# Table limits read from PSUM, second weights of expert 0 split later, gate copies deferred, and a new order of the first matmul groups

## The chip, the cores and the metric

The kernel runs on one core of a Trainium2 chip. The metric is the device time of one execution in microseconds; lower is better. TensorE (PE) does the matmuls, VectorE (DVE), ScalarE (ACT) and GpSimd (POOL) the work on elements, and SyncE (SP) issues most DMA transfers. Each engine goes through its own instructions in a fixed order and waits on semaphores for what other engines or DMA queues deliver.

## The reference, cut to what matters

Attention over 8 batches of 8 heads (576 tokens, head size 64) in which only scores within tau of the row's maximum are kept, then a mixture of 8 experts in which each of the 4608 tokens goes to one:

```python
scores = scale * np.matmul(q, k.transpose(0, 1, 3, 2))
thresh = np.max(scores, axis=-1, keepdims=True) - tau
scores = np.where(scores >= thresh, scores, -1000000000.0)
attn = softmax(scores)
x = (attn @ v), heads side by side            # 4608 x 512
logits = x @ w_gate                           # 4608 x 8
expert_idx = np.argmax(logits, axis=1)
for e in range(8):
    xe = x[expert_idx == e]
    h = np.maximum(xe @ w1[e], 0.0)           # 512 -> 1024
    out[expert_idx == e] = gate_w * (h @ w2[e])   # 1024 -> 512
```

## The kernel before

Everything large is held as a pair of 16-bit floats, a high part and a low part, and each product is made of three matmuls. A "split" writes the high part (ACT) and the low part (DVE: the value less its high part).

**Attention** goes through 32 pairs of heads, numbered n, each in 11 steps. In a step PE makes scores twice: `s` with tokens in rows (L356, L358), of which DVE takes the row maximum `nm` (L368), and for an earlier pair `st`, transposed (L404, L405), which ACT turns into `e` by the exponential (L421), DVE masks (L424), ACT rounds to `ph` (L429) and POOL takes the rest of into `pl` (L430). `av` (L474) multiplies `ph` and `pl` with the values `vop`. All `s` and `st` share six PSUM buffers, `av` has one, and one more PSUM buffer (tag "m") serves the small jobs. After four pairs, which are one batch, ACT copies the sums to `x` and `xh` (L484, L489), POOL normalises them (`xn`, L528), ACT and POOL split them into rows `R` (L535, L536), SP transposes `R` by DMA into `xTg` (L543), PE makes the logits `lg` (L561) and the ranks `rk` within an expert (L610 to L613), and POOL scatters the rows to a table `xs` in DRAM (L633, "put").

**Tables.** After batches 5, 6 and 7 `tables0`, `tables1` and `tables2` work out which rows of `xs` belong to which block of 128 tokens (m) of which expert. `counts` (L660) lets PE count the tokens (`pc`, a PSUM bank), DVE writes the counts less a base to `cnt` in SBUF (L665). `table_first` (L668) takes from `cnt` the limits `lim` (L681) and the flag `has` (L689), and works in the bank to the end, where `row` and `badi` come out as integers (L658).

**Experts.** `fetch(m)` gathers 128 rows by an indirect DMA of POOL (`Rm` or `R`<-`xs`, L847), has SP transpose them into `xTm` (L857), and copies the gate and the target of each row into `gt` (DVE L860, POOL L865). `gemm1` of a group of blocks makes `h` (L902) and ACT and DVE its split `hl` (L890, L891), `gemm2` makes `y` (L935); ACT scales it to `o` (L946), and POOL writes it out (L949). The blocks of expert 0 that `tables0` gives (m = 0, 1, 2) are computed as groups 0, 1, 2 while attention still goes on and right behind it; matmuls named h<-spare belong to group 3, which is made of spare rows. Weights come by SP (`wf`, L791) and are split by `split_w` (ACT L806, DVE L814). For expert 0 the low part of a weight goes through PE: a matmul with the identity puts the high part into PSUM (`hi_w`, L254), and DVE subtracts it from there (L255). Expert 0 has two `wf` buffers, the later ones eight, loaded from `close` on.

**Order.** `plan(k, f)` queues a piece for step k of attention, `after(d, f)` for d steps later, `moe(c, ready, f)` for chunk c of the expert work when a condition holds, and `hurry(f)` gives a piece's instructions high priority. A scheduler puts the instructions of each engine in order by priority and dependency. `experts` runs the groups: first weights of group i, then second weights of group i-1, and so on.

Of the kernel before, what the change touches and what calls it, by code (L numbers as in the profile page):

```python
# [50 lines left out]
def kernel(  # L51
# [123 lines left out]
    def plan(k, f, where=END):  # L175
        if urgent[0]:
            f = hurry(f)
        assert (k, where) >= (now[0], slot[0])
        acts.setdefault(k, ([], [], []))[where].append(f)
# [481 lines left out]
    def counts(nm):  # L661
        pc = ps_m.tile([P, 512], F32, tag="m", name=f"pc_{nm}")
        nc.tensor.matmul(pc[:, 0:E], ones, run, start=True, stop=True)
        c = tp.tile([P, E], F32, name=f"cnt_{nm}")
        nc.vector.tensor_tensor(c, pc[:, 0:E], base_e, ALU.subtract)  # L665
        return c, pc

    def table_first(nm, bank, cnt, start=None):  # L668

        bc = [P, E, NE]  # L670
        if start is None:
            rk_i = tp.tile(bc, I32, name="rk_i")
            nc.gpsimd.iota(rk_i, pattern=[[0, E], [P, NE]], base=0, channel_multiplier=1)
            nc.vector.tensor_copy(rk_f, rk_i)
        rk, bad = (bank[:, z:z + E * NE].rearrange("p (e n) -> p e n", e=E) for z in (32, 96))
        if start is None:
            nc.scalar.copy(rk, rk_f)
        else:
            nc.vector.tensor_tensor(rk, rk_f, start.unsqueeze(2).to_broadcast(bc), ALU.add)
        lim = tp.tile([P, E, 1], F32, name=f"lim{nm}")  # L680
        nc.vector.tensor_scalar(lim[:, :, 0], cnt, -1.0, None, ALU.add)  # L681
        nc.vector.tensor_tensor(bad, rk, lim.to_broadcast(bc), ALU.is_gt)
        nc.vector.tensor_scalar(bad, bad, float(1 << 20), None, ALU.mult)
        badi = to_int(bad, bc, f"badi{nm}")
        nc.vector.tensor_tensor(rk, rk, lim.to_broadcast(bc), ALU.min)
        nc.vector.tensor_tensor(rk, rk, base_e.unsqueeze(2).to_broadcast(bc), ALU.add)

        has = tp.tile([P, E, 1], F32, name=f"has{nm}")
        nc.vector.tensor_scalar(has[:, :, 0], cnt, 0.5, None, ALU.is_gt)  # L689
        nc.vector.scalar_tensor_tensor(rk, rk, pos0, has.to_broadcast(bc), ALU.subtract, ALU.mult)  # L690
        nc.vector.tensor_scalar(rk, rk, pos0, None, ALU.add)
        rowi = to_int(rk, bc, f"row{nm}")
        return rowi, badi
# [76 lines left out]
    groups += [(m, m + 1) for m in range(NPR, NEARLY, 2)]  # L770
    groups += [(m,) for m in range(NEARLY, NS)]
    group_of = {m: (g, i) for g in groups for i, m in enumerate(g)}
    ms = {}
    wq = {}
    T = {}
# [43 lines left out]
    def fetch(m):  # L819

        idx, bad, par = slots[m]
        g, i = group_of[m] if m != "x" else ((m,), 0)
        if m in range(NF, NF + 2):

            if "spare" not in T:
                T["spare"] = xp.tile([P, 2, NT * H * W // 2], F32, tag="x", name="spare")
            Rm = T["spare"][:, m - NF, 0:ROW].bitcast(I32)
            xT = T["spare"][:, m - NF, 520:1032].bitcast(F16).rearrange("p (i c t) -> p i c t", i=1, c=8)
        elif m in range(EARLY_SLOTS):
            Rm = pools[0].tile([P, ROW], I32, tag="Rm", name=f"Rm_{m}", bufs=2)  # L830
            xT = pools[0].tile([P, 1, 8, P], F16, tag="xTm", name=f"xTm_{m}", bufs=NF)
        else:
            Rm = R[:, 0 if m == "x" else m % 5]
            if i == 0:
                xT = rpool.tile([P, 2, 8, P], F16, tag="xT", name=f"xTm_{m}", bufs=3)
            else:
                xT = ms[g]["xT"]
        if i == 0:
            ms[g] = dict(xT=xT, par=par, gw=[], ti=[])
        d = ms[g]  # L840
        for z in range(1 + late(m)):
            dst = xT[:, i]
            if late(m):
                Rm = R[:, z if m == "x" else (2 * m + z) % 5]
                dst = xT.rearrange("p i c t -> p (i c t)")[:, 0:8 * PL].rearrange("p (c t) -> p c t", c=8)
                d["xT"], dst = dst, dst[:, :, P * z:P + P2 * z]
            get = nc.gpsimd.indirect_dma_start(  # L847
                Rm, None, xs[:, :], bass.IndirectOffsetOnAxis(ap=idx[:, z:z + 1].bitcast(U32), axis=0)
            )
            get = get.ins  # L850
            mine = [put for b, put in puts if b <= placed.get(m, B - 1)]
            for put in mine:
                tc.add_manual_dep(get, put.name, sync, reason="rows of the tokens placed so far")
            if m != "x":
                tc.declare_no_dep(get, group="puts", keep=mine, reason="rows of tokens placed later are others")
                tc.add_to_no_dep_group("gets", get)
            nc.sync.dma_start_transpose(dst, Rm[0:P2 if z else P, 0:DM].bitcast(F16))  # L857
            gt = small.tile([P, 2], I32, tag="gt", name=f"gt_{m}_{z}", bufs=6)
            gw, ti = gt.bitcast(F32)[:, 0:1], gt[:, 1:2]
            nc.vector.tensor_copy(gw, Rm.bitcast(F32)[:, DM:DM + 1])  # L860
            to = Rm[:, DM + 1:DM + 2]
            if z:
                nc.gpsimd.tensor_tensor(ti, to, to, ALU.add)
                to = ti
            nc.gpsimd.tensor_tensor(ti, to, bad[:, z:z + 1], ALU.add)  # L865
            d["gw"].append(gw)
            d["ti"].append(ti)

    def shape(g):

# [3 lines left out]
    def chunks(g):  # L874

        return 8 * shape(g)[1] // P

    def gemm1(g):
        d = ms[g]
        Wt, xT = wb1[d["par"]].rearrange("p c (h f) -> p c h f", h=2), d["xT"]  # L880

        n, w, per = shape(g)
        d["h"] = []

        def relu(ph, u):
            if u % 2 == 0:
                d["h"].append(ew.tile([P, 2, 2, 512], F16, tag="e", name=f"hl_{g[0]}_{u}"))
            h = d["h"][u // 2][:, :, u % 2, 0:per * w]
            ph = ph[:, 0:per * w]
            nc.scalar.activation(h[:, 0], ph, AF.Relu)  # L890
            nc.vector.scalar_tensor_tensor(h[:, 1], ph, 0.0, h[:, 0], ALU.max, ALU.subtract)  # L891

        for u in range(8 // per):
            ph = ps_sc.tile([P, 512], F32, tag="sc", name=f"h_{g[0]}_{u}")
            k = 0
            for q in range(per):
                f = slice((per * u + q) * P, (per * u + q + 1) * P)
                o = ph[:, q * w:(q + 1) * w]
                for c in range(4):
                    for z, (wh, xh) in enumerate(((0, 0), (0, 1), (1, 0))):  # L900
                        x = xT[:, 2 * c + xh] if late(g[0]) else xT[:, 0:n, 2 * c + xh]
                        nc.tensor.matmul(  # L902
                            o, Wt[:, c, wh, f], x, start=c == 0 and z == 0, stop=c == 3 and z == 2,
                        )
                        k += w
                        if k >= 12 * P and (q, c, z) != (per - 1, 3, 2):
                            k -= 12 * P
                            yield
            moe(chunk[0] + DH, lambda: True, lambda ph=ph, u=u: relu(ph, u))
            yield  # L910
# [3 lines left out]
    def gemm2(g):  # L914
        d = ms[g]
        Wt = wb2[d["par"]].rearrange("p c (a h d) -> p (c a) h d", a=2, h=2)
        n, w, per = shape(g)
        for i in range(len(d["ti"])):
            m = g[0] if late(g[0]) else g[i]

            half = late(m) and i
# [135 lines left out]

    def experts():

        for i in range(len(groups) + 1):  # L1060
            if i < len(groups):
                assert there(groups[i], 0)
                yield from gemm1(groups[i])
                past[0] = groups[i][-1]
            if i:
                assert there(groups[i - 1], 1)
                yield from gemm2(groups[i - 1])
                past[1] = groups[i - 1][-1]

    def room():  # L1070
        ldp.close()
# [11 lines left out]
    k = NSTEP * (NPAIR - 2) - LEAD - SL  # L1083
    plan(k + 1, room)
    for i in range(8):
        plan(k + WS0 + WSD * i, lambda i=i: split_w(*wseq[i]))
        if i + 2 < 8:
            plan(k + WS0 + WSD * i, lambda i=i: load_w(*wseq[i + 2]))
    TABLES = {B - 3: tables0, B - 2: tables1, B - 1: tables2}
    plan(KEND + 12, close)  # L1090


# [7 lines left out]

    at = []
    k = 0
    for i, g in enumerate(groups):
        at.append(k)
        k += chunks(g) + (chunks(groups[i - 1]) if i else 0)
    for i, g in enumerate(groups):
        for j, m in enumerate(g):
            if m >= NF + 2:
# [29 lines left out]
    def there(g, w):  # L1138

        e = g[0] // NE if g[0] < NEARLY else E + g[0] - NEARLY  # L1140
        return all((e, w, c) in split_done for c in range(4))
# [149 lines left out]
```

## Time and profile before

| | |
|---|---|
| three timed runs | 992.12, 993.51, 993.37 us; median 993.37 |
| profiled execution | 992.38 us |
| its span, first to last instruction | 990.7 us |
| PE busy | 939.0 us (95% of the span) |
| DVE, ACT, POOL busy | 702.8, 652.3, 561.6 us |
| mean granted PE clock | 0.987 of full |

Attention takes the span up to about 587 us; the expert work is woven into it from about 566 us and alone behind it. PE is busy nearly all the time, so what matters is where it is not: the start, the last fifty microseconds of attention, and the first seventy behind it.

### The profile page before, as it was taken

The numbers are of one execution on the slowest core, as the hardware profiler recorded it, in microseconds if no ns is written. First come the engines' busy times: TensorE is split into PE (matmuls) and PEld (weight loads), VectorE is DVE, ScalarE is ACT, GpSimd is POOL, SyncE is SP. The second block draws the span as 40 slices with busy tenths as digits, with TensorE's granted clock in tenths as the row PEclk, the third lists the DMA queues.
The fourth block names the chain that finished last, engine by engine and source line by source line (L and its number), as shares of the span: only waits on it lengthen the run. The fifth ranks groups of instructions, "written<-read, shape, count | busy, mean of one in ns | idle before, by whom it ended". The sixth has DMA issues, their size and how long they took to land. (4 is left out here: it accounts for less than half of the span.)

```text
span 990.7 us, 28651 instructions
## 1 busy us (share of the span) xinstructions
PE 939.0 (95%) x11548; PEld 604.1 (61%) x11548; DVE 702.8 (71%) x1413; ACT 652.3 (66%) x1111; POOL 561.6 (57%) x470
## 2 busy tenths in 40 slices
PE   7899999999999999999897898999999999999997
PEld 2355556556566556565564586777667766667684
DVE  7899999998999989999899875826243342423650
ACT  2689897997998889898988973534243342433651
POOL 6366886895996987978968871433122121221121
PEclk8899999999999999999999999999999999999999
DMA  6553554564564755646646639998574656556730
GB/s 199 143 132 80 146 134 125 140 164 112 127 179 115 162 125 141 171 94 170 152 97 188 149 104 289 363 228 250 164 232 115 216 151 180 171 155 209 224 105 27
DMA packets 142750, 159.20 MB, mean 161 GB/s; under 512 B 96403, under 2 KB 112789, under 8 KB 142614
## 3 DMA queue, kind: packets, MB, share of 16 engines
q1 hardware_dynamic: 126598, 100.33, 40.2%
q10 hardware_dynamic: 6768, 27.55, 8.9%
q0 software_dynamic: 9248, 29.45, 8.9%
q8 instruction: 92, 1.51, 0.7%
q14 instruction: 44, 0.36, 0.1%
HBM read 90.24 MB, written 19.44 MB: 111 GB/s over the span
## 5 line engine op out<-in xcount | busy, mean ns | idle before, releaser
L430 POOL TENSOR_TENSOR pl<-e,ph 128x1024 f16<-128x1024 f32 x158 | 335.9, 2134 | 105.1 <-ACT ph L429 66.6
L421 ACT ACTIVATE e<-st,ntau 128x512 f32<-128x512 f32 (+1 forms) x352 | 222.5, 650 | 54.2 <-PE st L405 51.5
L424 DVE SCALAR_TENSOR_TENSOR e<-st,e 128x512 f32<-128x512 f32 (+1 forms) x352 | 219.7, 635 | 12.2 <-ACT e L421 11.4
L935 PE MATMUL y<-wb,hl 128*128 128x512 f16 (+1 forms) x1056 | 201.8, 360 | 0.0
L368 DVE TENSOR_REDUCE nm<-s 128x1 f32<-128x512 f32 x300 | 188.1, 632 | 19.1 <-PE s L358 16.8
L902 PEld LDWEIGHTS <-wb 128*128 128x128 f16 x2304 | 188.2, 98 | 19.8 <-issue 1.2
L902 PE MATMUL h<-xTm,wb 128*128 128x256 f16 (+2 forms) x2112 | 195.2, 253 | 0.7 <-DMA xTm<-R 0.7
L474 PE MATMUL av<-vop,ph 128*128 128x65 f16 (+3 forms) x3072 | 187.7, 195 | 2.3 <-ACT x L484 2.0
L474 PEld LDWEIGHTS <-ph 128*128 128x128 f16 (+1 forms) x3072 | 158.3, 100 | 46.3 <-issue 21.3
L474 PE MATMUL av<-vop,pl 128*128 128x65 f16 (+1 forms) x1536 | 167.5, 194 | 4.6 <-POOL pl L430 4.5
L429 ACT CAST ph<-e 128x1024 f16<-128x1024 f32 x160 | 166.2, 1040 | 5.3 <-DVE e L424 5.0
L474 PEld LDWEIGHTS <-pl 128*128 128x128 f16 (+1 forms) x1536 | 136.6, 100 | 35.8 <-issue 10.5
L935 PEld LDWEIGHTS <-hl 128*128 128x128 f16 (+1 forms) x1056 | 94.0, 100 | 97.9 <-issue 1.9
L814 DVE SCALAR_TENSOR_TENSOR wb<-wf,wb 128x1024 f16<-128x1024 f32 x88 | 103.9, 1220 | 52.0 <-ACT wb L806 51.9
L404 PE MATMUL st<-QK 128*128 128x512 f16 (+3 forms) x640 | 138.8, 294 | 1.9 <-DVE lo L255 0.8
L405 PE MATMUL st<-CQ,ck 128*128 128x512 f16 (+3 forms) x640 | 137.4, 288 | 0.0
L356 PE MATMUL s<-QK 128*128 128x512 f16 (+1 forms) x600 | 129.6, 293 | 3.1 <-DMA QK<-hi 2.0
L358 PE MATMUL s<-ck,CQ 128*128 128x512 f16 (+1 forms) x600 | 128.0, 289 | 1.2 <-DMA CQ<-hi 1.2
L949 POOL DMA_INDIRECT out_dram<-o,gt x40 | 46.6, 1165 | 129.9 <-ACT o L946 118.8
L890 ACT ACTIVATE hl<-h 128x512 f16<-128x512 f32 (+1 forms) x80 | 45.6, 572 | 105.6 <-PE h L902 103.6
L806 ACT ACTIVATE wb<-wf 128x1024 f16<-128x1024 f32 x96 | 97.4, 1049 | 26.9 <-DMA wf<-in_w_dram 10.7
L860 DVE COPY gt<-R 128x1 f32<-128x1 f32 x33 | 5.1, 153 | 129.0 <-DMA out_dram<-o,gt 105.8
(194 smaller groups left out, 1016.6 us busy)
## 6 DMA issues: line engine op xcount, KB each, us to landing
wf<-in_w_dram SPq DMA_DIRECT2D x96, 512.0 KB
qkf<-in_qk_dram ACTq DMA_DIRECT2D x30, 576.0 KB
vf<-in_v_dram ACTq DMA_DIRECT2D x15, 640.0 KB
QK<-hi SPq DMA_DIRECT2D x64, 144.0 KB
QK<-lo SPq DMA_DIRECT2D x64, 72.0 KB
QK<-hi SPq DMA_DIRECT2D x64, 72.0 KB
ck<-lo SPq DMA_DIRECT2D x64, 72.0 KB
CQ<-hi SPq DMA_DIRECT2D x64, 64.0 KB
```

The costliest lines, as they stand in the source:

```text
L356: nc.tensor.matmul(sc[rows, oc], d["QA"][a][:, cols], d["KB"][a][:, CH[c]], start=True, stop=False)
L358: nc.tensor.matmul(sc[rows, oc], d["CQ"][:, at:at + cols.stop - cols.start], d["CK"][a][:, CH[c]], start=False, stop=True,)
L368: nc.vector.tensor_reduce(o, sc[:, 0:width(t)], axis=AX.X, op=ALU.max, negate=True)
L404: nc.tensor.matmul(sc[rows, oc], d["KB"][a][:, cols], d["QA"][a][:, CH[c]], start=True, stop=False)
L405: nc.tensor.matmul(sc[rows, oc], d["CK"][a][:, cols], d["CQ"][:, q], start=False, stop=True)
L421: nc.scalar.activation(pf, sc, AF.Exp, bias=ntau, scale=0.125 / SS)
L424: nc.vector.scalar_tensor_tensor(pf, sc, 0.0, pf, ALU.is_ge, ALU.mult)
L429: nc.scalar.copy(h, pd)
L430: (nc.vector if (n, t) in PLV else nc.gpsimd).tensor_tensor(l, pd, h, ALU.subtract)
L474: nc.tensor.matmul(av[:, 0:D] if z == 2 else av, l if z == 1 else h, vop[:, tv, W:W + D] if z == 2 else vop[:, tv, 0:W], start=i in (0, NT ...
L902: nc.tensor.matmul(o, Wt[:, c, wh, f], x, start=c == 0 and z == 0, stop=c == 3 and z == 2,)
L935: nc.tensor.matmul(o, h[:, hh], Wt[:, f, wh, c], start=f == 0 and z == 0, stop=f == 7 and z == 2)
```

## The change

Five edits:

1. `counts` writes the counts less the base into columns 8 to 15 of the PSUM bank, and ACT copies them to `cnt`. `lim` and `has` read the bank instead of `cnt`.
2. The four pieces of the second weights of expert 0 are split two steps apart from step KEND+1, behind the last pair's scores, instead of in attention. The loads of the last two pieces move with them. Low parts go through PSUM as before.
3. `tables0` is hurried.
4. The copies to `gt` are made later: 8 steps later for m below 5, otherwise 12 chunks later.
5. The groups run in the order `turns`: first weights of groups 0, 1 and 2, then second weights of 0 and 1, first of 3, second of 2, and then one by one as before.

```diff
@@ counts
-        nc.vector.tensor_tensor(c, pc[:, 0:E], base_e, ALU.subtract)
+        nc.vector.tensor_tensor(pc[:, 8:8 + E], pc[:, 0:E], base_e, ALU.subtract)
+        nc.scalar.copy(c, pc[:, 8:8 + E])
         return c, pc
@@ table_first
-        nc.vector.tensor_scalar(lim[:, :, 0], cnt, -1.0, None, ALU.add)
+        nc.vector.tensor_scalar(lim[:, :, 0], bank[:, 8:8 + E], -1.0, None, ALU.add)
...
-        nc.vector.tensor_scalar(has[:, :, 0], cnt, 0.5, None, ALU.is_gt)
+        nc.vector.tensor_scalar(has[:, :, 0], bank[:, 8:8 + E], 0.5, None, ALU.is_gt)
@@ groups
+    turns = [(1, 0), (1, 1), (1, 2), (0, 0), (0, 1), (1, 3), (0, 2)]
+    turns += [(w, i + w) for i in range(3, len(groups)) for w in (1, 0) if i + w < len(groups)]
@@ fetch
-            gt = small.tile([P, 2], I32, tag="gt", name=f"gt_{m}_{z}", bufs=6)
-            gw, ti = gt.bitcast(F32)[:, 0:1], gt[:, 1:2]
-            nc.vector.tensor_copy(gw, Rm.bitcast(F32)[:, DM:DM + 1])
...
+            def gates(Rm=Rm, z=z):
+                gt = small.tile([P, 2], I32, tag="gt", name=f"gt_{m}_{z}", bufs=6)
+                gw, ti = gt.bitcast(F32)[:, 0:1], gt[:, 1:2]
+                nc.vector.tensor_copy(gw, Rm.bitcast(F32)[:, DM:DM + 1])
...
+            if m == "x":
+                gates()
+            elif m < NF + 2:
+                after(8, gates)
+            else:
+                moe(chunk[0] + 12, lambda: True, gates)
@@ experts
-        for i in range(len(groups) + 1):
-            if i < len(groups):
-                assert there(groups[i], 0)
-                yield from gemm1(groups[i])
-                past[0] = groups[i][-1]
-            if i:
-                assert there(groups[i - 1], 1)
-                yield from gemm2(groups[i - 1])
-                past[1] = groups[i - 1][-1]
+        for first, i in turns:
+            assert there(groups[i], 1 - first)
+            yield from (gemm1 if first else gemm2)(groups[i])
+            past[1 - first] = groups[i][-1]
@@ weights of expert 0, tables
     for i in range(8):
-        plan(k + WS0 + WSD * i, lambda i=i: split_w(*wseq[i]))
+        t = k + WS0 + WSD * i if i < 4 else KEND + 1 + 2 * (i - 4)
+        plan(t, lambda i=i: split_w(*wseq[i]))
         if i + 2 < 8:
-            plan(k + WS0 + WSD * i, lambda i=i: load_w(*wseq[i + 2]))
-    TABLES = {B - 3: tables0, B - 2: tables1, B - 1: tables2}
+            plan(t, lambda i=i: load_w(*wseq[i + 2]))
+    TABLES = {B - 3: hurry(tables0), B - 2: tables1, B - 1: tables2}
```

DVE, where `tables0` begins during pairs 29 and 31. Names end in a number of the program, wb1_0 are the first weights of expert 0, and pc_0 is the bank of `tables0`. Before:

```order
L665 TENSOR_TENSOR cnt_0_12157<-pc_0_12155,base_e_109 128x8
L255 SCALAR_TENSOR_TENSOR wb1_0_11668<-wf_0_2_0_11829,hi_w0_2_0_12039 128x512
L255 SCALAR_TENSOR_TENSOR wb1_0_11668<-wf_0_2_0_11829,hi_w0_2_1_12051 128x512
L681 TENSOR_SCALAR lim0_12163<-cnt_0_12157 128x8
L689 TENSOR_SCALAR has0_12171<-cnt_0_12157 128x8
L368 TENSOR_REDUCE nm_31_11905<-s_31_5_12089 128x1
L255 SCALAR_TENSOR_TENSOR vop_1_128<-vf_15_11717,hi_v15_0_0_12093 128x5x64
```

Now:

```order
L665 TENSOR_TENSOR pc_0_12152<-pc_0_12152,base_e_109 128x8
L255 SCALAR_TENSOR_TENSOR wb1_0_11668<-wf_0_2_0_11829,hi_w0_2_0_12039 128x512
L255 SCALAR_TENSOR_TENSOR wb1_0_11668<-wf_0_2_0_11829,hi_w0_2_1_12051 128x512
L368 TENSOR_REDUCE nm_31_11905<-s_31_5_12089 128x1
L255 SCALAR_TENSOR_TENSOR vop_1_128<-vf_15_11717,hi_v15_0_0_12093 128x5x64
L255 SCALAR_TENSOR_TENSOR vop_1_128<-vf_15_11717,hi_v15_0_1_12100 128x5x64
L368 TENSOR_REDUCE nm_31_11905<-s_31_6_12110 128x1
L255 SCALAR_TENSOR_TENSOR wb1_0_11668<-wf_0_3_0_11915,hi_w0_3_0_12114 128x512
L424 SCALAR_TENSOR_TENSOR e_29_8_12001<-st_29_9_12071,e_29_8_12001 128x512
L682 TENSOR_SCALAR lim0_12161<-pc_0_12152 128x8
```

The limit reads PSUM, and stands six instructions later, behind two row maxima of pair 31; `has0` is not among these rows any more.

POOL, in the stretch behind that, up to the first gathers. Before:

```order
L528 TENSOR_TENSOR xn_6_3_12177<-x_6_10436,rs_6_11881 128x512
L430 TENSOR_TENSOR pl_29_8_12003<-e_29_8_12001,ph_29_8_12002 128x1024
L536 TENSOR_TENSOR R_129<-xn_6_2_12121,R_129 128x4x128
L430 TENSOR_TENSOR pl_29_4_12108<-e_29_4_12106,ph_29_4_12107 128x1024
L536 TENSOR_TENSOR R_129<-xn_6_3_12177,R_129 128x4x128
L430 TENSOR_TENSOR pl_29_6_12203<-e_29_6_12201,ph_29_6_12202 128x1024
L847 DMA Rm_0_12225<-xs_81,row0_12175 128x514
L847 DMA Rm_1_12272<-xs_81,row0_12175 128x514
L430 TENSOR_TENSOR pl_30_0_12335<-e_30_0_12333,ph_30_0_12334 128x1024
```

Now:

```order
L528 TENSOR_TENSOR xn_6_3_12175<-x_6_10436,rs_6_11881 128x512
L430 TENSOR_TENSOR pl_29_8_12003<-e_29_8_12001,ph_29_8_12002 128x1024
L430 TENSOR_TENSOR pl_29_4_12108<-e_29_4_12106,ph_29_4_12107 128x1024
L536 TENSOR_TENSOR R_129<-xn_6_2_12118,R_129 128x4x128
L536 TENSOR_TENSOR R_129<-xn_6_3_12175,R_129 128x4x128
L430 TENSOR_TENSOR pl_29_6_12201<-e_29_6_12199,ph_29_6_12200 128x1024
L430 TENSOR_TENSOR pl_30_0_12318<-e_30_0_12316,ph_30_0_12317 128x1024
L850 DMA Rm_0_12214<-xs_81,row0_12173 128x514
L850 DMA Rm_1_12258<-xs_81,row0_12173 128x514
```

The rest of pair 30's first scores, pl_30_0, now stands ahead of both gathers instead of behind them.

PE, where the logits of the last batch, lg_7, begin behind attention; h_2 and y_1 are the two products of groups 2 and 1, and lg_7 is made of five pieces of 12 matmuls. Before:

```order
L902 LDWEIGHTS wb1_0_11668
L902 MATMUL h_2_0_13474<-xTm_2_12351,wb1_0_11668 128x128
L561 LDWEIGHTS xTg_7_0_13425
L561 MATMUL lg_7_13511<-wg_107,xTg_7_0_13425 128x8
L561 LDWEIGHTS xTg_7_0_13425
```

Now:

```order
L947 LDWEIGHTS hl_1_0_13336
L947 MATMUL y_1_0_13630<-wb2_0_11669,hl_1_0_13336 128x512
L561 LDWEIGHTS xTg_7_0_13430
L561 MATMUL lg_7_13566<-wg_107,xTg_7_0_13430 128x8
L561 LDWEIGHTS xTg_7_0_13430
```

Between the end of attention's last av and lg_7 stood 84 matmuls h and 24 y, and the five pieces lay apart, with h and y between them. Now 144 h and 33 y stand ahead, and the five pieces follow each other.

## Rows read from the trace of the kernel before

**Rows 1.** The page: its first line, and busy time (share of span) and instructions of PE.

```profile
span 990.7 us, 28651 instructions
PE 939.0 (95%) x11548; PEld 604.1 (61%) x11548; DVE 702.8 (71%) x1413; ACT 652.3 (66%) x1111; POOL 561.6 (57%) x470
```

**Rows 2.** Windows: length, busy us per engine PE PEld DVE ACT POOL, clock, DMA share.

```profile
537.40:546.00 8.60, 4.58 (x14) 1.09 (x12) 8.60 (x13) 4.38 (x7) 6.96 (x7) 0.80 0.71 177
...
566.00:587.00 21.00, 21.00 (x491) 18.91 (x491) 13.57 (x34) 15.81 (x33) 16.15 (x12) 1.00 0.22 68
587.00:612.00 25.00, 22.39 (x301) 15.99 (x294) 15.04 (x32) 10.53 (x20) 7.17 (x10) 1.00 1.01 255
...
655.00:984.00 329.00, 329.00 (x2542) 229.65 (x2539) 127.54 (x168) 130.39 (x172) 75.80 (x96) 1.00 0.59 173
```

**Rows 3.** Waits of PE, 500 to 660 us: us in total, times, longest.

```profile
PE hi_w L254 <- DVE nm L368: 4.0, 1, 4.0
PE hi_w L254 <- ACT wb L806: 2.8, 3, 1.4
PE hi_v L254 <- ACT vop L286: 2.3, 1, 2.3
PE lg L561 <- DMA xTg<-R: 1.5, 3, 0.6
PE rk L610 <- DVE run L602: 1.1, 1, 1.1
PE h L902 <- DMA xTm<-R: 0.7, 1, 0.7
```

**Rows 4.** Timeline of DVE: start, us, engine, line, operation.

```profile
536.80 4.29 DVE L681 TENSOR_SCALAR lim<-cnt 128x8 f32<-128x8 f32 x1
...
547.46 0.17 DVE L658 CAST badi<-pc 128x32 int32<-128x32 f32 x1
```

**Rows 5.** Timeline of POOL; in brackets the idle time ahead and what ended it.

```profile
536.71 2.28 POOL L536 TENSOR_TENSOR R<-xn,R 128x512 f16<-128x512 f32 x2
538.94 2.12 POOL L430 TENSOR_TENSOR pl<-e,ph 128x1024 f16<-128x1024 f32 x1
...
542.50 2.05 POOL L528 TENSOR_TENSOR xn<-x,rs 128x512 f32<-128x512 f32 x2
546.30 2.13 POOL L430 TENSOR_TENSOR pl<-e,ph 128x1024 f16<-128x1024 f32 x1 [1.75 <-ACT ph L429]
548.54 1.16 POOL L536 TENSOR_TENSOR R<-xn,R 128x512 f16<-128x512 f32 x1
...
555.17 1.01 POOL L847 DMA_INDIRECT Rm<-xs,row  x1 [0.15 <-PE av L474]
```

**Rows 6.** Timeline of ACT.

```profile
543.66 0.69 ACT L421 ACTIVATE e<-st,ntau 128x512 f32<-128x512 f32 x1 [3.77 <-PE st L405]
...
549.31 1.06 ACT L806 ACTIVATE wb<-wf 128x1024 f16<-128x1024 f32 x1
```

**Rows 7.** Timeline of PE: the first h, and the end of attention.

```profile
565.69 0.38 PE L405 MATMUL st<-CQ,ck 128*128 128x512 f16 x1
565.90 0.83 PE L902 MATMUL h<-xTm,wb 128*128 128x128 f16 x12
...
587.19 2.85 PE L902 MATMUL h<-xTm,wb 128*128 128x128 f16 x48
589.88 5.34 PE L935 MATMUL y<-wb,hl 128*128 128x512 f16 x24
```

**Rows 8.** Timeline of SP, whose rows are DMA issues.

```profile
558.59 3.36 SPq L857 DMA_TRANSPOSE xTm<-Rm  x2
...
615.69 25.54 SPq L791 DMA_DIRECT2D wf<-in_w_dram  x15
643.88 6.72 SPq L857 DMA_TRANSPOSE xTm<-R  x2
```

**Rows 9.** A window as in the second group; the last but one number is the DMA share.

```profile
563.60:564.70 1.10, 1.10 (x34) 0.87 (x33) 0.93 (x6) 1.10 (x3) 1.08 (x3) 1.00 0.01 2
```

More of the change, by code (lines that the diff above doesn't have):

```diff
@@ L857, in fetch @@
             nc.sync.dma_start_transpose(dst, Rm[0:P2 if z else P, 0:DM].bitcast(F16))
-            gt = small.tile([P, 2], I32, tag="gt", name=f"gt_{m}_{z}", bufs=6)
-            gw, ti = gt.bitcast(F32)[:, 0:1], gt[:, 1:2]
-            nc.vector.tensor_copy(gw, Rm.bitcast(F32)[:, DM:DM + 1])
[L861 to L867, printed above, removed]
+            def gates(Rm=Rm, z=z):
+                gt = small.tile([P, 2], I32, tag="gt", name=f"gt_{m}_{z}", bufs=6)
+                gw, ti = gt.bitcast(F32)[:, 0:1], gt[:, 1:2]
+                nc.vector.tensor_copy(gw, Rm.bitcast(F32)[:, DM:DM + 1])
+                to = Rm[:, DM + 1:DM + 2]
+                if z:
+                    nc.gpsimd.tensor_tensor(ti, to, to, ALU.add)
+                    to = ti
+                nc.gpsimd.tensor_tensor(ti, to, bad[:, z:z + 1], ALU.add)
+                d["gw"].append(gw)
+                d["ti"].append(ti)
+            if m == "x":
[4 more added lines that the diff above has]
+                moe(chunk[0] + 12, lambda: True, gates)
     def shape(g):
@@ L917, in gemm2 @@
         n, w, per = shape(g)
-        for i in range(len(d["ti"])):
+        for i in range(2 if late(g[0]) else len(g)):
             m = g[0] if late(g[0]) else g[i]
@@ L1102 @@
     k = 0
-    for i, g in enumerate(groups):
-        at.append(k)
-        k += chunks(g) + (chunks(groups[i - 1]) if i else 0)
+    for begin, i in turns:
+        if begin:
+            at.append(k)
+        k += chunks(groups[i])
     for i, g in enumerate(groups):
```

## The prediction

> **What bounds the kernel now.** I read the page first: PE is busy for 939.0 of 990.7 us [rows 1], so at most 52 us are to be had, and the question is where they lie. The windows answer it. From 655 us to the end PE is busy in 329.00 of 329.00 us, and so it is in the last 21 us of attention [rows 2]: an edit that takes nothing from PE's own work gains nothing there. The idle time is in the stretch around 540 us (4.58 busy of 8.60) and right behind attention (22.39 of 25.00) [rows 2]. The list of PE's waits names what ended it: one wait of 4.0 us for a row maximum of DVE, 2.8 us in three waits for splits of weights by ACT, 2.3 us for ACT's split of the values; and behind attention 1.5 us in three waits for the transposed xTg, 1.1 us for the running counts and 0.7 us for a transposed xTm [rows 3]. The start-up, where PE also waits, is changed by one copy of a few elements, and I give it nothing.
>
> The 4.0 us have one origin. DVE's timeline shows `lim`, an operation on 8 elements per row, lasting 4.29 us from 536.80 to 541.09 [rows 4]. In all that time POOL works without a break, on two R and one pl, from 536.71 to 541.06 [rows 5], and `lim` ends when POOL ends. So it isn't working but held, by POOL. A DVE operation that reads PSUM isn't: the cast at 547.46 took 0.17 us while POOL was in a pl from 546.30 to 548.43 [rows 4, 5]. The row maxima queued behind `lim` then hold the shared PSUM buffers, PE can't write, and ACT stands for 3.77 us until 543.66 [rows 6]. PE pays a second time: its clock over 537.4 to 546 is granted at 0.80 of full [rows 2], so 40% of 8.6 us, 3.4 us, were at the lower of its two levels, 1.2 GHz; what it did in them would have taken half, so 1.7 us are lost.
>
> The Trainium skill ("SBUF — State Buffer", section "SBUF: two separate sides") says that VectorE and GpSimd share a pair of ports under a lock that is held for one whole instruction, the other blocking fully. Were the hold only to the end of the one POOL instruction under way, it would have ended within the first R, 1.2 us, and the edit would be worth 3 us less at this place; the trace shows it lasting across three instructions, 4.29 us, and I go by that.
>
> **The change part by part.**
>
> *Limits from PSUM.* `lim` now reads PSUM, like the cast: 0.17 us in place of 4.29 [rows 4]. Bounds: 0.17, and, if something else in it is held, what POOL's run leaves when it comes. It stands six instructions later, which would be about 540.0, so 1.1 us to 541.06. The added copies by ACT are on 8 columns, three in all. Bounds: nothing, and 0.69 us, the shortest ACT row that I show [rows 6]. I take some 0.2 us; the first falls into the time in which ACT waited 3.77 us. DVE, PE and ACT then go on some 3.8 us sooner, at PE's full clock.
>
> *Second weights behind the last pair.* This moves four ACT operations of 1.06 us [rows 6], 4.2 us at most; consecutive rows overlap by about a tenth, so I take 3.8 us; eight low parts on DVE; and eight PE matmuls of 512 columns, 5.34/24 = 0.22 each [rows 7], so 1.7 us. Two of PE's waits for splits (2.8 us in all, of which the first, for a first weight, stays) go with them, 2.0 us. ACT has room at the new place: 15.81 of 21.00 us busy [rows 2], so the 3.8 us are hidden; without that cover they would stand on the path of the last av. The 1.7 us are not hidden, since PE is full there; they come off the earlier stretch and go onto this one. The loads of the last two pieces need a buffer that the first two free. A load costs SP 25.54/15 = 1.70 us at its pace [rows 8], so each is ready some 3 us after the split that frees it, against some 6 us of matmuls that the new order puts between the first and the third on PE: 0 to 0.6 us of waiting, I take 0.3.
>
> *What is next late.* One would now add 4.0 + 1.7 + 2.0 + most of 2.3 us. I don't, because POOL comes next. Its 1.75 us of idleness ahead of 546.30 [rows 5] goes, but in the new order pl_30_0 stands ahead of the gather of Rm_0. From 542.50 to that gather there are now two xn (2.05), four pl (about 2.11 each), and two R (1.13 each) [rows 5]: 542.5 + 2.0 + 8.4 + 2.3 = 555.2, and 0.2 to 0.4 for issuing, so 555.5. Before it was at 555.17 [rows 5]. The gather gains nothing, it loses 0.3 us. Behind it comes the transposition: two issues of 1.68 each from 558.59 [rows 8], and all DMA is quiet from 563.6 [rows 9], so xTm_0 was there at about 563.6 - 1.7 = 561.9, which is 6.8 us after the gather began. Bounds: 5.1 (its issue ends at 560.27) and 8.4. So h_0_0 can start at 562.3 at the earliest, against 565.90 [rows 7]. PE itself, following ACT (3.8 us sooner, and 3.8 us of splits less, but some 2.6 us later at the logits of batch 6, which now stand ahead of av_29_1 and need an R that POOL, by the sum above, ends at 542.5 + 2.0 + 4.2 + 2.3 = 551.0), would be there at 565.9 - 5.0 = 560.9. So it waits for the gather, about 1.4 us. From h_0_0 to the end of av PE needed 587.19 - 565.90 = 21.3 us without a gap [rows 2, 7]; now 21.3 + 1.7 + 0.3 = 23.3. Attention ends at 562.3 + 23.3 = 585.6: **1.5 us sooner**, out of nine or so that the removed waits add up to.
>
> *The new order of groups.* Its worth is behind attention. Waits there: 1.5 + 1.1 + 0.7 = 3.3 us [rows 3]. That is counted from the modelled end of a matmul; each time PE restarts it also loses the overlap of one matmul with the next (0.38 long, but they follow at 0.22 [rows 7], so 0.16), five times, 0.8 us: 4.1 us. A few short ones add perhaps 0.3. Before lg_7 there are now 144 matmuls of h (2.85/48 = 0.059 each) and 33 of y (0.22) [rows 7]: 8.3 + 7.3 = 15.6 us behind the last av, against 84 and 24, 10.2 us. The longest wait for a piece was 0.6 us, and the pieces came some 2.4 us apart; SP's transposition of spare rows no longer stands between them. So all five have landed, or the last is a few tenths late. The ranks come 5 us later in PE's work than their cause, and y_6, 24 matmuls, stands ahead of h_7, 5.3 us for a wait of 0.7. I take **4.1 us** of the 4.4.
>
> *Hurried tables, deferred gates.* The copies to `gt` are a few short ones on DVE and POOL; nothing on PE's path waits for them before y leaves. They are worth nothing at either place; the cover is that DVE and POOL are free for 5 to 7 us of the last 21 [rows 2]. The hurry lets `row` be ready sooner, but POOL is not.
>
> *Sum:* 1.5 + 4.1 = 5.6 us. The profiled execution took 992.38 us, 1.0 less than the median of the runs, 993.37; I set the sum against the middle, 992.9: **987.3 us**. Against its own time it would be 986.8.
>
> **The rivals.** *A: the gather isn't binding.* If POOL's chain closes up more, or the row lands at the lower bound (5.1 us behind the gather), ACT sets the end: h_0_0 at 560.9 rather than 562.3, and with ACT ahead of PE to the end another 0.9. Then 7.9 us: 985.0. For it: ACT loses 7.6 us of waiting and work; against it: the gather's place behind pl_30_0. Chance 0.17.
>
> *B: the second weights come late.* Only two buffers hold them, so two loads follow two splits one for one. If both are waited for behind attention, 2 x 1.70 = 3.4 us [rows 8] go: a gain of 2.2 us, 990.7. For it: transposes of Rm share SP's queue with the loads; against it: PE is 6 us away. Chance 0.18.
>
> *C: the limit is held all the same*, because it still writes SBUF. Then 1.1 us are lost at the place where it stands now: 988.4. Against it: the cast, which also writes SBUF [rows 4]. Chance 0.08.
>
> *D: slower than before.* The transposes of block 7 (6.72 us for two, from 643.88) follow 25.54 us of loads on SP [rows 8]; in the new order two more loads and four loads of registers stand ahead of them. Two loads cost 3.4 us; the register loads wait for `tables3`. h_7 waited 0.7 us before and has 5.3 us more cover now, so it waits again from 4.6 us on, and the kernel is slower from 4.6 + 5.6 + 2 = 12 us of delay on. It would be 995 or more. The Trainium skill ("PSUM — Partial Sum Buffer", section "PSUM bank collisions raise a hardware error") has a rule that speaks for delay here: two engines may not touch one bank at a time, so software orders them. Each `lim` now waits for ACT's copy out of the same bank, which no row of before shows; at ACT's own queue that is one operation, about a microsecond, far from twelve. Chance 0.07.
>
> **How the numbers follow.** The forecast 0.50, A 0.17, B 0.18, C 0.08, D 0.07. Of the three timed runs the extremes lie 1.4 us apart, so 0.2%, 2 us, is about what can be told from no change. The forecast, A, C and a bit over half of B are faster by more than that: 0.85. The rest of B and the mildest of D are the same: 0.09; 0.06 is slower. The range goes from A less its landing bound (984.2) to B with the spread of runs (991.0).
>
> **What would show it.** In the new profile `lim` should take 0.2 us, PE should have no wait of 4 us for `nm`, and the clock from 540 to 546 should be full. The gather of Rm_0 should start at about 555.5 and h_0_0, waiting for xTm, at 562.3. The last av should end at 585.6, and the windows behind it should show less than 0.5 us idle up to 655 us. I am wrong if h_0_0 doesn't wait, if a wait for wb of more than 1 us stands among the last av, if lg_7 waits by more than 1 us, or if h_7 waits longer than 0.7 us.

## The result and the profile after

The changed kernel is slower: 1002.6 us median of 11 runs (996.72 to 1005.26), against 994.41 us for 11 runs of before beside them. The ratio is 1.0074, 95% interval 1.0056 to 1.0092: some 7 us lost, where 5.6 us of gain were forecast. The profiled execution took 1003.65 us. Its page begins:

```profile
span 1001.9 us, 28665 instructions
PE 947.5 (95%) x11548; PEld 608.8 (61%) x11548; DVE 698.0 (70%) x1413; ACT 653.6 (65%) x1114; POOL 561.7 (56%) x470
```

Windows of after, columns as in [rows 2]:

```profile
537.40:546.00 8.60, 6.72 (x51) 2.54 (x49) 8.60 (x21) 7.86 (x15) 8.40 (x8) 1.00 0.90 208
546.00:558.00 12.00, 8.74 (x168) 6.42 (x165) 6.62 (x22) 7.62 (x16) 11.52 (x8) 0.77 0.41 78
...
566.00:587.00 21.00, 18.57 (x402) 16.42 (x399) 13.45 (x24) 15.63 (x31) 13.22 (x10) 0.99 0.42 124
587.00:612.00 25.00, 22.02 (x280) 15.44 (x278) 15.15 (x40) 9.02 (x18) 6.16 (x8) 0.84 0.77 179
...
655.00:984.00 329.00, 326.01 (x2458) 227.00 (x2456) 129.96 (x178) 129.49 (x170) 72.08 (x96) 0.99 0.60 177
```

Around 540 us the change did what it says: PE is busy for 6.72 of 8.60 us instead of 4.58, at full clock. But the last 21 us of attention are no longer full (18.57 busy), the clock is low in the stretches from 546 to 558 (0.77) and from 587 to 612 (0.84), and behind 655, where nothing was idle, 3 us are. PE's waits of after from 500 to 670 us, to be held against [rows 3]:

```profile
PE lg L561 <- DMA xTg<-R: 4.4, 3, 1.5
PE hi_w L254 <- ACT wb L809: 3.3, 3, 2.4
PE h L914 <- issue: 2.6, 6, 0.8
PE av L474 <- POOL pl L430: 1.5, 2, 1.3
PE hi_v L254 <- ACT vop L286: 1.3, 1, 1.3
```

The 4.0 us for a row maximum are gone. New is `issue`, a wait in which the profile shows nothing that is waited for; from 600 to 680 us it comes to 4.7 us in eight pieces:

```profile
PE h L914 <- issue: 4.7, 8, 1.0
```

Before had none. One place, on PE's timeline of after, and what POOL issued just ahead of it and during it:

```profile
666.99 2.00 PE L914 MATMUL h<-xTm,wb 128*128 128x128 f16 x33
669.82 0.38 PE L914 MATMUL h<-xTm,wb 128*128 128x128 f16 x4 [0.82 <-issue]
671.23 0.44 PE L914 MATMUL h<-xTm,wb 128*128 128x128 f16 x5 [1.03 <-issue]
672.66 3.54 PE L914 MATMUL h<-xTm,wb 128*128 128x128 f16 x37 [0.99 <-issue]
```

```profile
664.09 0.99 POOL L850 DMA_INDIRECT R<-xs,row  x1 [0.15 <-issue]
665.38 0.97 POOL L850 DMA_INDIRECT R<-xs,row  x1 [0.30 <-issue]
666.66 0.95 POOL L850 DMA_INDIRECT R<-xs,row  x1 [0.30 <-issue]
667.91 0.95 POOL L850 DMA_INDIRECT R<-xs,row  x1 [0.30 <-DVE gt L865]
669.17 1.01 POOL L961 DMA_INDIRECT out_dram<-o,gt  x1 [0.30 <-issue]
```

PE gets four or five matmuls, stands for a microsecond, gets the next few. The other place is 628.1 to 631.7 us (waits of 0.35 to 0.55 us), while POOL scatters the five pieces of batch 7 from 622.18 on. In before the five gathers of this kind ran from 636.40 to 644.3 us, and PE was in 24 matmuls of 512 columns from 637.75 until 642.93. In after the clock is at 0.50 of full, the lower level, over 553 to 559, 587 to 590, 608 to 614 and 673 to 675 us. Only the last of these stretches stands behind issue waits; the others stand behind waits of 1.3 to 2.4 us for data.

### The profile page after: what moved, and what is told of

Same layout as the page of the kernel before. It is cut to its first block, busy times and chain, and to the rows that moved or that the text cites. A ratio compares the mean times of both kernels' runs of the same rounds, so it can differ in the third digit from the quotient of the medians.

```text
span 1001.9 us, 28665 instructions
## 1 busy us (share of the span) xinstructions
PE 947.5 (95%) x11548; PEld 608.8 (61%) x11548; DVE 698.0 (70%) x1413; ACT 653.6 (65%) x1114; POOL 561.7 (56%) x470
## 5 line engine op out<-in xcount | busy, mean ns | idle before, releaser
L958 ACT ACTIVATE o<-y,gt 128x512 f32<-128x512 f32 (+1 forms) x40 | 26.5, 664 | 98.3 <-PE y L947 81.9
```

## The experiments

All were timed beside before, in five rounds (burst in three, after_again once). "Last av" is where the last av starts in the profiled execution; "issue" sums PE's issue waits from 535 us on; the clocks are means over 535 to 590 and 590 to 700 us. A mean clock of c over T us costs at most (1 - c) x T.

The last av's time by itself misleads, since the executions are apart before any moved piece runs. ACT's `rs` of batch 6 stands ahead of all of them; in before, lim_alone and half_old_spaced it started at

```profile
523.40 0.25 ACT L513 ACTIVATE rs<-x 128x32 f32<-128x32 f32 x1
...
520.22 0.25 ACT L513 ACTIVATE rs<-x 128x32 f32<-128x32 f32 x1
...
519.71 0.25 ACT L513 ACTIVATE rs<-x 128x32 f32<-128x32 f32 x1
```

though lim_alone's order is still that of before there. So two columns are added: the time from this `rs` to the last av, and from the last av to the end of the span. They rest on one profile each, and differences of about 1 us in them are not told apart. lim_alone, lim_spaced and w2_early have 24 more h ahead of the last av than the others, 1.4 us of PE's work.

| run | ratio to before (95%) | last av | rs to last av | behind it | issue | clocks |
|---|---|---|---|---|---|---|
| before | | 587.1 | 63.7 | 403.6 | 0 | 0.97, 1.00 |
| after | 1.0074 (1.0056 to 1.0092) | 588.8 | 66.4 | 413.1 | 4.7 | 0.91, 0.95 |
| after_again | | 584.7 | 65.2 | 416.7 | 5.3 | 0.94, 0.94 |
| lim_alone | 1.0010 (0.9991 to 1.0030) | 584.5 | 64.3 | 409.2 | 3.0 | 1.00, 0.97 |
| w2late_alone | 1.0047 (1.0022 to 1.0072) | 588.6 | 66.4 | 407.3 | 1.3 | 0.90, 0.97 |
| w2_early | 1.0016 (0.9997 to 1.0035) | 589.7 | 66.2 | 407.2 | 5.0 | 0.97, 0.98 |
| old_turns | 1.0115 (1.0073 to 1.0157) | 584.6 | 65.4 | 416.4 | 9.0 | 0.94, 0.94 |
| burst | 1.0068 (1.0039 to 1.0098) | 586.4 | 66.2 | 416.2 | 6.9 | 0.94, 0.95 |
| w2_half | 1.0014 (0.9996 to 1.0032) | 582.7 | 62.7 | 407.5 | 3.6 | 0.97, 0.97 |
| sbuf_lim | 1.0053 (1.0022 to 1.0084) | 588.5 | 67.6 | 406.9 | 0.5 | 0.87, 0.97 |
| half_old | 0.9988 (0.9963 to 1.0013) | 588.0 | 63.8 | 407.1 | 4.0 | 0.94, 0.98 |
| half_mid | 1.0019 (0.9994 to 1.0045) | 582.5 | 62.7 | 412.0 | 6.3 | 0.94, 0.97 |
| half_spaced | 0.9983 (0.9963 to 1.0003) | 580.9 | 62.7 | 405.9 | 0.9 | 0.97, 0.98 |
| half_old_spaced | 0.9962 (0.9941 to 0.9983) | 582.3 | 62.6 | 405.6 | 0.5 | 0.94, 0.97 |
| after_spaced | 1.0027 (1.0011 to 1.0043) | 590.3 | 67.4 | 407.5 | 0 | 0.91, 0.98 |
| before_spaced | 1.0000 (0.9980 to 1.0020) | 583.9 | 64.1 | 404.6 | 0 | 0.97, 0.98 |
| lim_spaced | 1.0009 (0.9994 to 1.0023) | 587.0 | 63.6 | 405.3 | 0 | 1.00, 0.97 |

**One part at a time.** My first theory was that the second weights come too late; rivals were the order of the groups and the tables.

```diff
# lim_alone: before, with
-        nc.vector.tensor_tensor(c, pc[:, 0:E], base_e, ALU.subtract)
+        nc.vector.tensor_tensor(pc[:, 8:8 + E], pc[:, 0:E], base_e, ALU.subtract)
+        nc.scalar.copy(c, pc[:, 8:8 + E])
...
# w2late_alone: before, with
+        t = k + WS0 + WSD * i if i < 4 else KEND + 1 + 2 * (i - 4)
...
# w2_early: after, with
-        t = k + WS0 + WSD * i if i < 4 else KEND + 1 + 2 * (i - 4)
+        t = k + WS0 + WSD * i
...
# old_turns: after, with
+    turns = [t for i in range(len(groups) + 1) for t in ((1, i), (0, i - 1)) if 0 <= t[1] < len(groups)]
```

> The kernel before with the first edit alone (limits and flag read PSUM, ACT copies the counts). Theory 1 (the loss comes from the second weights, which are now loaded and split too late): this part is harmless, lim takes 0.2 us, PE's wait of 4.0 us for a row maximum goes, and the kernel is 3 to 6 us faster than before. Theory 2 (the loss comes from the new order of the groups, with all of lg_7 in one piece): the same, 3 to 6 us faster. Theory 3 (the chain of tables2 through ACT is late): slower than before by some us, with a wait of h_7 or of a neighbour for xTm.

> The kernel before with the second edit alone (second weights of expert 0 split behind the last pair). Theory 1: 1 to 5 us slower than before; PE waits 2 us or more for wb among the last av, and the clock falls behind it; the 4.0 us wait for the row maximum stays. Theory 2: within 2 us of before, since lg_7 still lies apart. Theory 3: within 2 us of before.

> The changed kernel with the second edit undone (second weights split in attention again). Theory 1: the loss is gone, 8 to 12 us faster than the changed kernel, so 2 to 5 us faster than before; no wait of over 1 us for wb among the last av. Theory 2: lg_7 still waits for 3 us; 2 to 5 us faster than the changed kernel, so still slower than before. Theory 3: as slow as the changed kernel.

> The changed kernel with the fifth edit undone (groups in the order of before). Theory 1: the wait of 2.4 us for wb and the low clock behind it stay; at most 4 us faster than the changed kernel, so 4 us slower than before. Theory 2: the waits of lg_7 shrink below 1 us in all and the kernel is 6 us or more faster than the changed one. Theory 3: as slow as the changed kernel.

w2late_alone lost about 4.7 us by itself, as theory 1 said, and w2_early is some 6 us better than the changed kernel. By its profile under 2 us of this lie in attention (from rs to the last av 66.2 us, 64.8 without the 24 more h, against 66.4), the rest behind it. old_turns is no faster than the changed kernel (the intervals overlap), so putting the order of the groups back undoes nothing. But lim_alone gained nothing, against all theories: its wait of 4.0 us is gone and its clock full, yet from rs to the last av it took 64.3 us (62.9 without the 24 more h) against 63.7. In each of the four profiles stood issue waits, most in the slowest. That gave theory C: PE's instructions come late where POOL issues indirect transfers in a row while PE runs short matmuls. "Late instructions" is from here on a name for the issue waits; what PE stands for in them no run shows.

**The suspected cost by itself**, the first edit undone, two of the four late pieces undone, and the changed kernel once more:

```diff
# burst: before, with this behind the last relu of groups 3 and 14
+        for i in range(5):
+            nc.gpsimd.indirect_dma_start(
+                T["dummy"][:, i], None, rows, bass.IndirectOffsetOnAxis(ap=own[:, 1:2].bitcast(U32), axis=0)
+            )
...
# w2_half: after, with
-        t = k + WS0 + WSD * i if i < 4 else KEND + 1 + 2 * (i - 4)
+        t = k + WS0 + WSD * i if i < 6 else KEND + 1 + 2 * (i - 6)
...
# sbuf_lim: after, with lim_alone's lines as in before
```

> The kernel before with two bursts of five small gathers (128 rows of 256 bytes, read from the weights into a spare tile; nothing uses them): one in POOL's order behind the rows of batch 7 and ahead of the gathers of block 7 on, so during first-weight matmuls of single blocks (128 columns), and one far behind, at group 14, where matmuls have 256 and 512 columns. Theory C (PE's instructions come late when POOL issues indirect transfers in a row while PE runs short matmuls): PE shows waits named issue of 1 us or more between 630 and 650, in pieces of four matmuls, none at the second burst, and 1 to 4 us are lost. Rival (the issue waits come from the place in the program or from the loads of weights): no such wait, the time within 1 us of before.

> The changed kernel with two of the four second-weight pieces split in attention again and two behind the last pair. Both late pieces then sit in the two buffers long before they are split, no load follows a split. Theory L (PE waits for wb because the load of the third piece can start only when the first has been split): no wait for wb of over 0.6 us among the last av, clock full there, the last av at 585 to 587, 4 to 8 us faster than the changed kernel. Rival (ACT is too full at that place, whatever the loads): a wait of 1 to 2.4 us for wb stays, at most 2 us faster than the changed kernel.

> The changed kernel with the first edit undone: limits and flag read the copy in SBUF. If holding lim is worth what the prediction says, lim takes several us again where POOL works, PE waits for a row maximum again, and the kernel is 3 to 6 us slower than the changed one. Rival (what the first edit gains is lost again behind attention): within 2 us of the changed kernel, or faster.

> The changed kernel once more, for a second profile. If the waits named issue and the low clock belong to the program, they stand at the same instructions (near 627 and 669 us; low clock near 552, 587, 607 and 672); if they belong to one execution, they stand elsewhere or are gone.

burst lost 6.8 us. PE's timeline of burst, during the five added gathers of 630.73 to 637.8 us and the five of before, which follow at once:

```profile
633.16 2.84 PE L916 MATMUL h<-xTm,wb 128*128 128x128 f16 x48
636.46 0.22 PE L916 MATMUL h<-xTm,wb 128*128 128x128 f16 x1 [0.46 <-issue]
637.18 0.27 PE L916 MATMUL h<-xTm,wb 128*128 128x128 f16 x2 [0.50 <-issue]
...
643.75 0.69 PE L916 MATMUL h<-xTm,wb 128*128 128x128 f16 x5 [0.83 <-issue]
645.21 0.58 PE L916 MATMUL h<-xTm,wb 128*128 128x128 f16 x4 [0.77 <-issue]
646.61 1.54 PE L916 MATMUL h<-xTm,wb 128*128 128x128 f16 x13 [0.82 <-issue]
```

48 matmuls run at 0.06 us each, then the same work trickles, and the clock falls. At the second burst, among matmuls of 256 and 512 columns, PE has no wait at all. The loss exceeds the 1 to 4 us that I expected; with the gathers of before it is ten in a row, not five.

w2_half removed the wait among the last av, as theory L said: attention took 62.7 us from rs, against 66.4 and 65.2 in the two profiles of the changed kernel, and by the ratios it is 6.0 us faster. sbuf_lim wasn't slower than the changed kernel though `lim` took 4.28 us and the 4.0 us wait for a row maximum is back: the rival held. What the first edit gains in attention is lost behind it: sbuf_lim has 0.5 us of issue waits where the changed kernel has 4.7, and is 6 us shorter behind the last av (406.9 against 413.1). after_again has its issue waits and low clocks at nearly the same places (issue at 626 to 629 and 667 to 670 us; 550 to 557, 605 to 611 and 670 to 676 at the lower clock), so they belong to the program. It was 2.9 us ahead of after at rs already and ended at the same time: behind the last av it took 3.6 us longer.

**From the other side**: the order of before, a third order, and room between the gathers.

```diff
# half_old: w2_half with the turns of old_turns;  half_mid: w2_half with
+    turns = [(1, 0), (1, 1), (0, 0), (1, 2), (0, 1), (0, 2), (1, 3)]
...
# *_spaced: in fetch, from block 3 on, two fills of a 128x512 tile on POOL between one gather and the next
+                if "last" in T:
+                    tc.add_manual_dep(get, T["last"], sync, reason="room between gathers")
+                for _ in range(2):
+                    rest = tc.keep_in_program_order(nc.gpsimd.memset(room_t, 0.0))
+                T["last"] = rest.ins.name
```

> As w2_half (two second-weight pieces early), and the order of groups of before. The gathers of the spare rows, which start some 2 us behind the last av, then fall on y_0 (512 columns) instead of on 144 matmuls of 128 columns in a row. Theory C (late instructions where gathers in a row meet short matmuls): the issue waits near 588 us (2.7 us in w2_half) go; 1 to 4 us faster than w2_half, so faster than before by 1 to 4 us. Rival (the new order of groups is good by itself, since lg_7 no longer waits): lg_7 waits for xTg by 1.5 us or more again, and the kernel isn't faster than w2_half.

> As half_old, but with second weights of group 2 ahead of first weights of group 3, so that the ranks of batch 7 stand behind 512-column work. Theory W (what is left there is PE's wait for the running counts, 1.1 to 1.8 us): that wait goes; about 1 us faster than half_old. Theory C: the rows of batch 7 are then scattered while PE runs h_3 and h_4 of 128 columns for 10 us, so issue waits of 1 to 4 us appear at about 620 to 630 us and the gain is lost, 0 to 3 us slower than half_old.

> As w2_half, with two fills of a small tile on POOL behind each gather from block 3 on, so that the gathers don't follow each other at 1.3 us. Theory C: issue waits near 588 and 660 us shrink below 0.5 us in all, 1 to 4 us faster than w2_half. Rival (the gathers don't matter, the place in the program does): the issue waits stay at 3 us or so, the time within 1 us of w2_half.

> half_old and the spaced gathers together. Theory C: no issue waits behind attention at all, as fast as the faster of half_old and half_spaced or 1 us better, so 2 to 5 us faster than before. Rival: the later gathers make first weights wait for xTm by 1 us or more, and it is no faster than half_old.

In half_mid the wait for the running counts is gone, as theory W said, but the scatter of batch 7 and the gathers behind it now meet matmuls of 128 columns: 6.3 us of issue waits at 622 to 624 and 643 to 649, as theory C said, and by the ratios it is 3 us slower than half_old (the intervals overlap). The fills, which only add work, cut the issue waits from 3.6 to 0.9 us and from 4.0 to 0.5, and by the ratios both kernels became faster by some 3 us; from rs to the end the profiles shrank by 1.6 and 2.7 us. half_old_spaced is faster than before by 0.38%, its interval clear of 1, and faster than the changed kernel by 1.1%. Its profile doesn't show the gain over before where the edits are: from rs to the end it took 468.2 us against 467.3. Its waits from 535 us on begin with the transposes of batch 7, which still leave something to be had:

```profile
PE lg L561 <- DMA xTg<-R: 4.8, 1, 4.8
PE hi_w L254 <- ACT wb L809: 1.6, 2, 1.2
```

**The shares.** The same fills in the changed kernel, in before and in lim_alone:

> The changed kernel with the two fills behind each gather from block 3 on, and nothing else. If late instructions of PE are a part of its loss, the issue waits shrink from some 5 us to below 2 (those at the scatter of batch 7, near 627 us, are not touched by the fills), and it is 2 to 5 us faster than the changed kernel, 3 to 6 us slower than before: the late second weights and the low clock stay. If they only take the place of other waits, it is within 1.5 us of the changed kernel.

> The kernel before with the same fills. Its own profile shows no issue wait, so by theory C nothing is to be had: within 2 us of before, or slower by a wait for a later gather. Rival (the fills help by themselves, whatever the edits): 2 us or more faster, like half_old_spaced.

> lim_alone (the first edit alone) with the same fills. lim_alone lost 3.0 us to issue waits near 645 us. Theory C: these go, and what the first edit gains in attention, 2 to 3 us, is left: 2 to 4 us faster than before. Rival (the gain is lost to lg_7's transposes, not to late instructions): within 1.5 us of before.

In the changed kernel they bring the ratio from 1.0074 to 1.0027: the fills win back about 4.7 of the 7.4 us lost (give or take 2.4 by the two intervals). This is a net figure: all issue waits went, with them the low clock at 673 us, but y's waits for weights grew from 0.4 to 2.4 us. The issue waits at the scatter of batch 7 went too, where no fills stand, against what I expected. In before, which has no issue waits, the fills bring nothing, so they don't help by themselves; whether half_old_spaced owes its gain to the edits with the fills the profiles, as said, don't show. In lim_alone the issue waits went and the ratio did not change; PE's waits of lim_spaced from 587 to 660 us are one line, and the tile's own view names what ended it, a transpose:

```profile
PE lg L561 <- DVE xn L528: 5.1, 1, 5.1
...
  DMA xTg<-R: 5.3, 1
```

The rival's time held: the wait for the transposes of batch 7, among which SP has those of spare rows, took the place of the issue waits. Without the 24 more h, lim_spaced took 62.2 us from rs to the last av and lim_alone 62.9, against before's 63.7: alone, the first edit is worth about 1 us there, not the 4.0 us of its wait. From rs to the end lim_spaced's profile is 4.6 us shorter than lim_alone's (468.9 against 473.5), which the twelve runs of each don't show; that stays open.

## Why the prediction was wrong

**Right.** `lim` took 0.15 us while POOL was in a pl, and PE's 4.0 us wait and the low clock at 540 went. POOL was next: the gather of Rm_0 began at 554.35 us (555.5 forecast), and the first h at 562.36 (562.3), waiting for xTm, though PE was there only just before it (after was 1 us ahead of before at rs, so both are about 1 us later than these numbers look):

```profile
537.98 2.13 POOL L430 TENSOR_TENSOR pl<-e,ph 128x1024 f16<-128x1024 f32 x1
...
539.32 0.15 DVE L682 TENSOR_SCALAR lim<-pc 128x8 f32<-128x8 f32 x1
...
554.35 1.02 POOL L850 DMA_INDIRECT Rm<-xs,row  x1 [0.16 <-issue]
...
562.36 0.83 PE L914 MATMUL h<-xTm,wb 128*128 128x128 f16 x12 [0.21 <-DMA xTm<-Rm]
```

**First failed step: the second weights.** "each is ready some 3 us after the split that frees it ... I take 0.3." The buffer isn't free with ACT's split: the low part reads it too, through PE and DVE. On the timelines of after the first split ends at 576.37, DVE's four low parts run from 577.63 to 580.2, SP issues the load at 578.97, and ACT and PE wait for it:

```profile
577.63 2.58 DVE L255 SCALAR_TENSOR_TENSOR wb<-wf,hi_w 128x512 f16<-128x512 f32 x4
...
578.97 8.35 SPq L794 DMA_DIRECT2D wf<-in_w_dram  x3
...
584.35 1.06 ACT L809 ACTIVATE wb<-wf 128x1024 f16<-128x1024 f32 x1 [3.17 <-DMA wf<-in_w_dram]
...
585.45 0.59 PE L254 MATMUL hi_w<-wb,ident_h 128*128 128x512 f16 x2 [2.37 <-ACT wb L809]
```

The load landed 5.3 us after its issue, where I had put the 1.70 us of SP's pace. So 8.0 us instead of 3, a wait of 2.37 us instead of 0.3 (1.59 in after_again), and half the clock from 587 to 590. From the first h to the last av PE took 26.5 us instead of the 23.3 forecast. Attention, forecast 1.5 us shorter, took 2.7 us more than before from rs on, 1.5 more in after_again. Rival B had the two buffers and the late loads, at 3.4 us, and still on the faster side.

**Second failed step: "4.1 us of the 4.4" behind attention.** This is the larger one: behind the last av 4.1 us were to be gained, and after took 9.5 us more than before (413.1 against 403.6), after_again 13.1. The five pieces of lg_7 stand together, so the first late one stops everything: 1.45 and 1.53 us for the last two, where "a few tenths" were allowed. SP had put a load between the transposes:

```profile
592.75 5.86 SPq L543 DMA_TRANSPOSE xTg<-R  x3
598.71 0.52 SPq L794 DMA_DIRECT2D wf<-in_w_dram  x1
599.90 2.70 SPq L543 DMA_TRANSPOSE xTg<-R  x2
...
607.18 0.48 PE L561 MATMUL lg<-wg,xTg 128*128 128x8 f16 x12 [1.45 <-DMA xTg<-R]
609.20 0.48 PE L561 MATMUL lg<-wg,xTg 128*128 128x8 f16 x12 [1.53 <-DMA xTg<-R]
```

And 4.7 us of issue waits came up, a wait of which the rows of before show none and which no term or rival has. The 144 matmuls of 128 columns in a row are not by themselves the cause: old_turns, in the order of before, has 9.0 us of issue waits, and sbuf_lim, with the 144, has 0.5. Where they come depends on which of POOL's bursts meets which matmuls, and every edit moves that; by what rule, the runs show only in part (last section).

**Third failed step: the clock.** The prediction takes the 1.7 us lost at 540 as gone and puts no new low clock into any term. By the windows the low clock costs at most 0.03 x 55 = 1.7 us in before and 0.09 x 55 + 0.05 x 110 = 10.5 us in after (clocks over 535 to 590 and 590 to 700). In after the stretch from 552 us follows four waits of 1.34, 0.54, 1.34 and 1.38 us between 544 and 554 us, which together replace the one of 4.0; that from 587 follows the wait for wb, that from 607 the waits of lg_7, that from 672 three issue waits of 0.8 to 1.0 us. So these waits were paid for twice. Not every wait is: behind the 2.27 us of before at 557 us and behind the issue waits of after at 628 to 632 us the clock stays full.

**The rivals.** A didn't come about (h_0_0 waited, if only 0.21 us), nor did C. D had the sign, not the cause: the transposes of block 7 were issued at 654.77 us, 11 us later than before [rows 8], as it feared, but no h waited for them. 5.6 us were forecast as gain, 7.4 us were lost. How these 13 us divide among late weights, lg_7, issue waits and the clock behind each isn't settled: undoing half of the second edit (w2_half) wins 6.0 us, the fills (after_spaced) 4.7, and the two overlap. A slip in the working carries nothing: 144 times 0.059 is 8.5 us, not 8.3. The upper end of the range, 991.0, is only 0.3 us above rival B's 990.7, less than the spread of 1.4 us that it names.

## What to carry to other kernels

When a stall is removed, ask not only what is late next, but which bursts of gathers will now meet which matmuls. Room of a microsecond between the gathers was worth some 3 to 5 us in three kernels with issue waits, and nothing in lim_alone and in before. A buffer is free when its last reader is done, and the last reader of a weight can be on the third engine from the one that seems to use it. A row of before prices only the waits that before has. And before two profiles are compared by the time at which something ended, they should be lined up at an instruction ahead of the change: at `rs` of batch 6 the profiles here were up to 6 us apart.

## What the runs showed of the hardware

PE can stand with no wait that the profile shows: one to five matmuls of 128 columns, then 0.3 to 1.5 us of nothing, mostly from the third to fifth indirect transfer on that POOL issues at about 1.3 us (in half_old and w2_half also at the 8-column logits, behind two gathers). Among the 512-column matmuls of before (637.75 to 643 us) and at the second burst there was none (in old_turns one of 0.45 us stands at the last y of five), and with some 1.1 us of fills between the gathers hardly any. But a meeting of the two isn't enough. In before the last two of five scatters (617.41 to 624.33 us) meet h, which starts at 621.85, without a wait. In sbuf_lim four gathers from 589.72 us meet h, with the clock at 0.50 until 595, and none comes either:

```profile
590.74 10.64 PE L913 MATMUL h<-xTm,wb 128*128 128x128 f16 x144
```

The Trainium skill ("Runtime: NRT & Kernel Launch", section "Instruction fetch mechanics") says that an engine's instructions are fetched in blocks by a DMA queue of its own and that the cost is mostly hidden. Before shows no issue wait. That those of after are this cost no run shows, and one sign speaks against it: the profile names two DMA queues "instruction", and neither moves a packet in after from 627.5 to 632 us or from 662 to 675 us, around the two groups of waits. From 662 to 675 us only these queues are listed:

```profile
q0 software_dynamic: 560, 1.84, 44.1%
q1 hardware_dynamic: 3814, 0.94, 38.2%
```

So no packet of theirs ended these waits, and what PE stands for stays open.

A DVE operation held by POOL stayed held over three of POOL's instructions, 4.29 us [rows 4, 5]; in sbuf_lim, which has it read SBUF again, it took 4.28 us, and reading PSUM 0.15 to 0.29 us.
